# Channel weights loaded as four whole rows per partition, with the contraction index taken as 4p+c

## The chip, the cores and the metric

The kernel runs on one core of one Trainium2 chip. The metric is device time of one execution in microseconds (us), and the time given for a kernel is the median of its runs. Times of single instructions come from one profiled execution and are counted from the start of its span.

## The reference

Two layers follow each other. The first is a linear attention with 8 batches, 8 heads, 576 positions and 64 channels a head. The second takes its output as x with 8 x 576 x 512 elements, mixes the lowest 64 frequencies of every channel with complex weights of their own, and ends in a product over channels:

```python
q_p, k_p = (phi(q), phi(k))                       # phi(x) = elu(x) + 1
kv = np.einsum('bhsd,bhse->bhde', k_p, v)
z = np.sum(k_p, axis=2)
num = np.einsum('bhsd,bhde->bhse', q_p, kv)
den = np.einsum('bhsd,bhd->bhs', q_p, z)[..., None] + 1e-06
x = num / den                                     # heads side by side: [8, 576, 512]

X = np.fft.rfft(x, axis=1)
Yr = np.einsum('bmd,mde->bme', Xr, w_r) - np.einsum('bmd,mde->bme', Xi, w_i)   # m < 64
Yi = np.einsum('bmd,mde->bme', Xr, w_i) + np.einsum('bmd,mde->bme', Xi, w_r)
y = np.fft.irfft(Y, n=S, axis=1)
u = x + y
return u + np.maximum(u @ w_ch, 0.0)              # w_ch: [512, 512]
```

The mode weights w_r and w_i are 64 x 512 x 512 float32 each, 134 MB in all. The channel weights w_ch are 512 x 512 float32, 1 MB. This document is about how w_ch lies in the on-chip memory.

## The kernel before

**Stages.** From 0 to about 112 us the kernel loads q, k and v, forms the attention for each batch (`turn_q`, `sum_kv`, `form_x`), and takes the Fourier transform of x as a product with a table (`transform`, L349), with the result placed by `place_x` for the mode products. From then on it walks through 32 pairs of modes (`mode_pair`, L465; the last one is `last_pair`, L490). Pair p multiplies by its weights in 16 matmuls (`product`, L432, into PSUM tile P), copies P to the f16 tile ys (`evacuate`, L447, on VectorE for even p and on ScalarE for odd p), and turns ys into rows of modes with four matmuls against a small table pick_sb (`picks`, L455). The pieces of ys, 128 columns each, are the stationary operand there.

**Weights.** The mode weights come through GpSimd's DMA queue, with a cast from float32 to bfloat16, 1 MB written for each half of a pair (`w_load`, L119; `w_load_last`, L131, in smaller pieces). Five pairs have buffers of their own at the start; later ones share two buffers, so the load of pair p+2 is issued when the product of pair p is done. The channel weights are loaded once, by L529, on the same queue behind the first five pairs, with a cast to float16, into wch16: `[128, 4, 512]`, 128 partitions of 4 pieces. The table pick_sb follows it (L531).

**Other work between the products.** The list `work` holds the rest in a fixed order, and `work_slot` takes so many items of it in the middle and at the end of each pair; `share` says how many. The instructions are pinned to the order of the program (`pin`). For each tile t of 128 rows, `fold` adds the inverse transform of the first 32 modes to x and writes a float16 copy x16w; `turn_x` (L698) transposes it in four pieces of 128 channels into xTw; `channel_product` (L707) multiplies xTw with wch16 and keeps the result as E0. For later modes, `early_rows` (L665), `form_z` (L728), `form_y` (L739) and `ahead_rows` (L920) turn the transposed spectrum into rows (y) and into rows times w_ch (z), and `fold_lead` uses the first two batches' rows. `keep_warm` (L419) adds matmuls whose result nobody reads.

**The end.** `last_pair` multiplies the very last mode the other way round (L518): its weights are the stationary operand, in 32 pieces of 128 columns, and the result y_last lands transposed. After that, L978 to L989 transpose the last rows of y (into last_y, halves copied by ScalarE at L979 and VectorE at L980) and form z, L990 and L767 add the inverse transform to all tiles, ScalarE takes the maximum with zero, VectorE adds, and the rows are stored.

**The index that the change concerns.** In every product with wch16 the 512 contracted channels are split into four pieces of 128. Before, piece c holds channels 128c to 128c+127, and partition p of piece c holds channel 128c + p. Where a transposed operand is made, it takes 128 adjacent columns; where rows are made from it, the four pieces are put side by side.

Of the kernel before, what the change touches and what calls it, by code (L numbers as in the profile page):

```python
# [43 lines left out]
def kernel(  # L44
# [10 lines left out]
    nc = tc.nc  # L55
# [5 lines left out]
    NDC = D // 128  # L61
    NJJ = 4
    NDW = 4 * NDC
    NDL = NDW // 2
# [6 lines left out]
    RA = 2 * B * NA  # L71
# [11 lines left out]
    id16 = const.tile([128, 128], F16, name="id16")  # L83
    fwd_sb = const.tile([128, 5, 2 * NM], F16, name="fwd_sb")
    pick_sb = const.tile([128, 32], F16, name="pick_sb")
    wch16 = const.tile([128, NDC, D], F16, name="wch16")
# [21 lines left out]
    pin = tc.keep_in_program_order  # L108
    PIECES = (slice(0, 2), slice(2, 4), slice(4, 6), slice(6, 7), slice(7, 8))
    HALVES = [slice(0, 64), slice(64, 128)]  # L110

    LAST = NM // 2 - 1

    def w_load(p: int, half: int, pool, tag: str, bufs: int):
        if half == 0:
            w_in[p] = pool.tile([128, NDW, D], BF16, tag=tag, bufs=bufs, name=f"w{p}")
        two = (moe_w_r, moe_w_i)[half][2 * p : 2 * p + 2]
        pin(
            nc.gpsimd.dma_start(  # L119
                out=w_in[p][half::2], in_=two.rearrange("g (r dc) e -> (g r) dc e", dc=NDW)  # L120
            )
        )

    def w_load_last(pool, tag: str, bufs: int):
        w_in[LAST] = pool.tile([128, NDW, D], BF16, tag=tag, bufs=bufs, name=f"w{LAST}")
        for g in range(2):
            for half in range(2):
                rows_in = (moe_w_r, moe_w_i)[half][NM - 2 + g].rearrange("(p dc) e -> p dc e", dc=NDL)
                for dcs in PIECES if (g, half) == (1, 1) else (slice(0, NDL),):
                    dst = w_in[LAST][half::2, g * NDL + dcs.start : g * NDL + dcs.stop]  # L130
                    pieces.append(pin(nc.gpsimd.dma_start(out=dst, in_=rows_in[:, dcs, :])))  # L131
# [279 lines left out]
    def w_get(p: int):  # L411
        if p not in w_in and p == LAST:
            w_load_last(wpool, "w", W_KEEP)
        elif p not in w_in:
            for half in range(2):
                w_load(p, half, wpool, "w", W_KEEP)
        return w_in[p]
# [9 lines left out]
    def work_slot(p: int, name: str):  # L427
        for _ in range(slots.get((p, name), 0)):
            if work:
                work.pop(0)()  # L430

    def product(P, x, n: int, w, dc: int, n_dc: int):  # L432
        c = dc % NDC * 32
        pin(
            nc.tensor.matmul(  # L435
                P[c : c + n, :], x, w[:, dc, :],
                start=(dc < NDC), stop=(dc >= n_dc - NDC), tile_position=(0, c),
                skip_group_check=True,
            )
        )  # L440

    def set_diagonal(p: int):
        for h in range(2):
            src = xt_v[HALVES[h], :, :, :, p].rearrange("p c t b -> p c (t b)")
            pin(nc.vector.tensor_copy(out=xz[p % 2][HALVES[h], :, h, :], in_=src))  # L445
# [9 lines left out]
    def picks(kk: int, st, n: int):  # L455
        for ec in range(NDC):
            pin(
                nc.tensor.matmul(  # L458
                    yt_ps[:, ec, kk % 8 : kk % 8 + n, :].rearrange("p m n -> p (m n)"),
                    st[:, ec * 128 : ec * 128 + 128],  # L460
                    pick_sb[:, 0 : n * 2 * B],
                )
            )

    def mode_pair(p: int):  # L465
# [5 lines left out]
        for dc in range(NDW):  # L471
            product(P, xz[p % 2][:, dc].rearrange("p h n -> p (h n)"), 32, w, dc, NDW)
        if p + 1 < LAST:
            set_diagonal(p + 1)
# [15 lines left out]
    def last_pair():  # L490
        xl = ystage.tile([128, NDL, 2 * B], BF16, name="xl")
        for h in range(2):
            src = xt_v[:, (2 * h + 1) * NDC : (2 * h + 2) * NDC, :, :, LAST]
            pin(
                nc.vector.tensor_copy(
                    out=xl[:, h * NDC : h * NDC + NDC], in_=src.rearrange("p c t b -> p c (t b)")
                )
            )
        w = w_get(LAST)
        kk = NM - 2  # L500
        ahead_rows()
        work_slot(LAST, "start")
        P = psW.tile([128, D], F32, tag="P", bufs=2, name=f"P{kk}")
        for dc in range(NDL):
            n = 32 if dc < NDC else 2 * B
            product(P, xt_cols(dc, kk, n), n, w, dc, NDL)
        st = evacuate(kk, P)
        work_slot(LAST, "mid")
        picks(kk, st, 1)
        pin(nc.vector.tensor_copy(out=Y8[:, :, NA, :], in_=yt_ps[:, :, NA, :]))  # L510
        ahead_gathers()
        keep_warm(3)
        y_last = psW.tile([128, NDC, 2 * B], F32, tag="P", bufs=2, name="y_last")
        for piece in PIECES:
            for dc in range(piece.start, piece.stop):
                for ec in range(NDC):
                    pin(
                        nc.tensor.matmul(  # L518
                            y_last[:, ec, :], w[:, NDL + dc, ec * 128 : ec * 128 + 128], xl[:, dc, :],
                            start=(dc == 0 and ec == 0), stop=(dc == NDL - 1), skip_group_check=True,  # L520
                        )
                    )
            keep_warm(WARM[piece.stop])
        nc.vector.tensor_copy(out=Y8[:, :, NL - 1, :], in_=y_last)

    while pending:
        w_next()
    tc.keep_in_program_order(
        nc.gpsimd.dma_start(out=wch16, in_=moe_w_ch.rearrange("(c p) j -> p c j", p=128))  # L529
    )  # L530
    tc.keep_in_program_order(nc.gpsimd.dma_start(out=pick_sb, in_=pick_dr.ap()))  # L531
    psA_ctx.close()
# [18 lines left out]
    rows = [Y8[:, ec].rearrange("p m n -> p (m n)") for ec in range(NDC)]  # L551
# [38 lines left out]
    YZ = [YZ_all[:, b] for b in range(B)]  # L590
# [74 lines left out]
    def early_rows(b: int):  # L665

        r = 2 * NF
        y_ps = bank(f"ye{b}", [128, NDC, 128], F16)
        for ec in range(NDC):
            yt = YE_T[:, ec].rearrange("p m (t b) -> p (m t) b", b=B)[:, :, b]  # L670
            pin(nc.tensor.transpose(y_ps[:r, ec, :], yt, id16))
        YE[b] = ye_slots()[:, b % 2, :]
        pin(nc.vector.tensor_copy(out=YE[b][:r], in_=y_ps[:r].rearrange("p c r -> p (c r)")))

    ye_at: list = []

# [21 lines left out]
    def turn_x(t: int):  # L698

        x16 = x16w.pop(t)  # L700
        xT_ps = bank(f"xTp{t}", [128, NDC, 128], F16)
        for c in range(NDC):
            pin(nc.tensor.transpose(xT_ps[:, c, :], x16[:, c * 128 : c * 128 + 128], id16))  # L703
        xTw[t] = sW.tile([128, NDC, 128], F16, tag="xTw", bufs=2, name=f"xTw{t}")
        pin(nc.vector.tensor_copy(out=xTw[t], in_=xT_ps))  # L705

# [32 lines left out]
    def form_y(b: int):  # L739

        y_ps = bank(f"yp{b}", [128, NDC, 128], F16)
        for ec in range(NDC):
            pin(nc.tensor.transpose(y_ps[:, ec, :], late_rows(ec, b), id16))
        pin(nc.vector.tensor_copy(out=YZ[b][:, 0, :], in_=y_ps.rearrange("p c r -> p (c r)")))

    def fold_lead(t: int):

# [170 lines left out]
    ahead = sW.tile([128, 2, D], F16, tag="rows", bufs=1, name="rows_ahead")  # L918

    def ahead_rows():  # L920

        pin(nc.vector.tensor_copy(out=Y8[:, :, 0:NA, :], in_=yt_ps[:, :, 0:NA, :]))
        ya_ps = psW.tile([128, NDC, 128], F16, tag="P", bufs=2, name="ya_ps")
        za_ps = psW.tile([128, D], F32, tag="P", bufs=2, name="za_ps")
        for ec in range(NDC):
            pin(nc.tensor.transpose(ya_ps[:, ec, :], rows[ec], id16))
        for ec in range(NDC):
            pin(
                nc.tensor.matmul(
                    za_ps, rows[ec], wch16[:, ec, :], start=(ec == 0), stop=(ec == NDC - 1)  # L930
                )
            )
        pin(nc.scalar.copy(out=ahead[0:RA, 0, :], in_=ya_ps[0:RA].rearrange("p c r -> p (c r)")))
        pin(nc.scalar.copy(out=ahead[0:RA, 1, :], in_=za_ps[0:RA]))

    def late_at(h: int, r0: int, n: int):
# [23 lines left out]
    for n in range(N_PRE):  # L960
# [4 lines left out]
    last = [  # L965
        sW.tile([128, D], F16, tag="x16w", bufs=2, name="last_y"),
        sW.tile([128, NDC, 128], F16, tag="xTw", bufs=2, name="last_z").rearrange("p c r -> p (c r)"),
    ]
    z1_ps = psW.tile([128, NDC, 8, 2 * B], F32, tag="yt", bufs=1, name="z1l")
    y_ps = [  # L970
        psW.tile([128, NDC, 128], F16, tag="P", bufs=2, name=f"ypl{h}")[:, 0 : NDC // 2] for h in range(2)
    ]
# [3 lines left out]
    COLS = [slice(h * hw, h * hw + hw) for h in range(2)]  # L976
    for ec in range(NDC):
        pin(nc.tensor.transpose(y_ps[ec // 2][:, ec % 2, :], rows[ec], id16))  # L978
    pin(nc.scalar.copy(out=last[0][:, COLS[0]], in_=y_ps[0].rearrange("p c r -> p (c r)")))  # L979
    pin(nc.vector.tensor_copy(out=last[0][:, COLS[1]], in_=y_ps[1].rearrange("p c r -> p (c r)")))  # L980
    for h in range(2):
        for ec in range(NDC):
            pin(
# [25 lines left out]
    def sums_of(n: int, tiles_of):  # L1009
        channels(n, tiles_of)  # L1010
        add_inverse(n, 1, tiles_of)
        for i in tiles_of:
# [6 lines left out]
            out=x_of(0), in0=accs[0][:, 0], scalar=0.0, in1=x_of(0), op0=ALU.max, op1=ALU.add  # L1019
# [50 lines left out]
```

## Time and profile before

| What | Value |
|---|---|
| Median of 3 runs | 420.76 us (420.64 to 420.87) |
| The profiled execution | 421.02 us; span of its instructions 419.2 us |
| TensorE matmul busy | 313.1 us, 75% of the span |
| VectorE busy | 231.2 us, 55% |
| ScalarE busy | 155.1 us, 37% |
| GpSimd's DMA queue (casting loads) | 12,688 packets, 81.54 MB, 93.6% of 16 engines' span |
| Read from HBM | 163.93 MB |
| L529, the load of w_ch | 512 KB written; issue 782 ns at 86.88 us; 37.7 us from issue to landing |
| Loads of mode weights, 1 MB written each | 13.1 us (w_r) and 17.5 us (w_i) from issue to landing, at the median |

A line of a group names the source line, the engine, the operation, output and inputs, their shapes, the count, the total busy time and the mean of one in ns, and then how long the engine stood idle before such instructions and what ended that. PE is a matmul and PEld the load of its stationary operand; loads overlap the matmuls before them. A line of the chain or of the timeline starts with the time in us and the duration. The time from a DMA's issue to its landing includes what is queued ahead of it.

### The profile page before, as it was taken

To read this page: it belongs to the slowest core of one execution; us is meant where nothing else is said; L and a number is where in the kernel's file an instruction comes from. 1 tells how busy PE (TensorE), PEld (TensorE's weight loads), DVE (VectorE), ACT (ScalarE), POOL (GpSimd) and SP (SyncE) were. 2 spreads that over 40 slices of the span, in tenths; PEclk is the share of its full clock that TensorE was granted. 3 is DMA by queue.
4 is the path that set the end of the run, shared out by engine and by line. 5 is a ranking of instruction groups with operands and counts; after the bars stand their busy time and mean duration, and the time that the engine had idled before them with its cause. 6 is when DMAs were issued, how large, how long until landed. Compare 5 with 4: busy or idle time off the path is not lost.

```text
span 419.2 us, 7479 instructions
## 1 busy us (share of the span) xinstructions
PE 313.1 (75%) x3143; PEld 162.6 (39%) x3143; DVE 231.2 (55%) x511; ACT 155.1 (37%) x255; POOL 59.1 (14%) x104
## 2 busy tenths in 40 slices
PE   0369997999607774777666686988788877998993
PEld 0257775877301331223222233333333323363421
DVE  4588899695414572464645353464446443532794
ACT  4687797854201020000000233344353423231783
POOL 4222224210011211111111111111111111130200
PEclk9999998579855687555856599899999989799998
DMA  8999999999999999999999999999999999999698
GB/s 217 212 212 217 209 224 203 228 208 222 213 227 205 223 219 208 224 217 209 220 216 214 220 209 220 217 212 220 220 208 220 217 213 220 213 202 177 229 394 331
DMA packets 17229, 93.17 MB, mean 222 GB/s; under 512 B 2284, under 2 KB 3196, under 8 KB 13036
## 3 DMA queue, kind: packets, MB, share of 16 engines
q0 software_dynamic: 12688, 81.54, 93.6%
q1 hardware_dynamic: 4508, 11.16, 7.2%
q8 instruction: 24, 0.39, 0.3%
q14 instruction: 9, 0.07, 0.0%
HBM read 163.93 MB, written 9.44 MB: 414 GB/s over the span
## 4 chain that ended last, share of the span: by engine, by line
DMA 60%; PE 24%; DVE 6%; issue 3%; ACT 3%; POOL 3%; DVEq 0%; ACTq 0%; POOLq 0%
DMA w<-in_moe_w_i_dram 48%; DMA pick_sb<-row_pick 8%; PE P L435 7%; DMA k<-in_k_dram 3%; PE acc L767 3%; PE kvp L260 2%; PE zl L422 2%; PE acc L807 2%; PE eps L713 2%; DVE x L296 1%; POOL w L119 1%; PE z L733 1%; ACT ke L211 1%; PE yb L752 1%; ACT qT L247 1%
## 5 line engine op out<-in xcount | busy, mean ns | idle before, releaser
L435 PE MATMUL P<-w,xz 128*32 128x512 bf16 x496 | 42.9, 479 | 39.2 <-DMA w<-in_moe_w_i_dram 37.0
L452 ACT CAST ys<-P 128x512 f16<-128x512 f32 x15 | 8.8, 586 | 133.7 <-PE P L435 133.7
L422 PE MATMUL zl<-wch,id 128*128 128x512 f16 x177 | 55.9, 466 | 0.0
L119 POOL DMA_DIRECT2D w<-in_moe_w_r_dram x31 | 17.1, 552 | 247.8 <-PE P L435 222.1
L450 DVE CAST ys<-P 128x512 f16<-128x512 f32 x17 | 11.8, 692 | 51.6 <-PE P L435 51.6
L713 PE MATMUL eps<-wch,xTw 128*128 128x512 f16 x144 | 39.7, 402 | 0.0
L435 PEld LDWEIGHTS <-xz 128*32 128x32 bf16 x496 | 12.5, 108 | 64.4 <-DMA w<-in_moe_w_i_dram 40.9
L166 PEld LDWEIGHTS <-qT 64*128 64x128 f16 (+1 forms) x640 | 22.6, 122 | 30.7 <-issue 16.0
L696 ACT CAST x16w<-x_main 128x512 f16<-128x512 f32 x32 | 19.8, 618 | 37.4 <-DVE x_main L694 37.4
L694 DVE TENSOR_TENSOR x_main<-ya,x_main 128x512 f32<-128x512 f32 x32 | 22.0, 689 | 18.4 <-PE ya L690 18.2
L260 PE MATMUL kvp<-vpad,ke 32*128 32x130 f16 x576 | 24.3, 261 | 8.9 <-ACT qT L247 6.0
L445 DVE COPY xz<-xt_c 64x256 bf16<-64x256 bf16 x62 | 23.0, 372 | 11.2 <-PE P L435 10.4
L721 ACT CAST E<-eps 128x512 f16<-128x512 f32 (+1 forms) x40 | 21.2, 540 | 19.0 <-PE eps L713 19.0
L422 PEld LDWEIGHTS <-id 128*128 128x128 f16 x177 | 18.2, 113 | 24.3 <-issue 13.8
L260 PEld LDWEIGHTS <-ke 32*128 32x128 f16 x576 | 22.1, 115 | 10.6 <-issue 8.1
L166 PE MATMUL nw<-kv_sb,qT 64*128 64x65 f16 (+1 forms) x320 | 17.9, 230 | 10.1 <-DVE x_tail L657 4.7
L296 DVE TENSOR_TENSOR x<-num,rd 128x512 f16<-128x512 f32 x32 | 22.1, 692 | 1.1
L240 PE MATMUL qTp<-id,qe 128*128 128x128 f16 x144 | 14.1, 276 | 11.5 <-DVE qe L224 9.5
L458 PE MATMUL yt<-pick_sb,ys 128*128 128x32 f16 (+1 forms) x128 | 8.6, 183 | 17.3 <-DMA pick_sb<-row_pick 9.7
L705 DVE COPY xTw<-xTp 128x512 f16<-128x512 f16 x36 | 15.0, 416 | 11.5 <-PE xTp L703 11.4
L657 DVE TENSOR_TENSOR x_main<-nw,rd 128x256 f32<-128x256 f32 x32 | 11.2, 416 | 17.6 <-PE nw L166 17.6
L211 ACT ACTIVATE qe<-q 128x1152 f16<-128x1152 f16 (+1 forms) x16 | 17.9, 1157 | 8.3 <-DMA q<-in_q_dram 8.2
(129 smaller groups left out, 509.1 us busy)
## 6 DMA issues: line engine op xcount, KB each, us to landing
w<-in_moe_w_r_dram POOLq DMA_DIRECT2D x31, 1024.0 KB, 13.1
w<-in_moe_w_i_dram POOLq DMA_DIRECT2D x31, 1024.0 KB, 17.5
out_dram<-x_main SPq DMA_DIRECT2D x12, 512.0 KB, 3.7
k<-in_k_dram POOLq DMA_DIRECT2D x8, 576.0 KB, 12.8
v<-in_v_dram POOLq DMA_DIRECT2D x8, 576.0 KB, 14.5
q<-in_q_dram POOLq DMA_DIRECT2D x7, 576.0 KB, 12.6
out_dram<-x_main SPq DMA_DIRECT2D x8, 256.0 KB, 3.0
q<-in_q_dram SPq DMA_DIRECT2D x2, 576.0 KB, 4.5
```

Of the source, the lines that this page charges most:

```text
L119: nc.gpsimd.dma_start(out=w_in[p][half::2], in_=two.rearrange("g (r dc) e -> (g r) dc e", dc=NDW))
L166: mm = nc.tensor.matmul(num[hpo][orow, c0 : c0 + 65], qT[rows, hpp, h2, cols], kv_sb[rows, hpp, h2, :])
L211: pin(nc.scalar.activation(out=ev[:, c], in_=heads(nm, b, c), func=AF.Exp))
L260: nc.tensor.matmul(kv_ps[:, h2, 0:130], phi["k", b][r0 : r0 + 32, j // NJ, j % NJ].rearrange("p o d -> p (o d)"), vp[r0 : r0 + 32, :, j, 0 ...
L296: nc.vector.tensor_tensor(out=dst.rearrange("p (o c d) -> p o c d", o=2, c=4), in0=nv[:, :, :, 0:64], in1=rden.unsqueeze(3).broadcast_to([ ...
L422: pin(nc.tensor.matmul(last_ps[0], id16, wch16[:, 0, :]))
L435: nc.tensor.matmul(P[c : c + n, :], x, w[:, dc, :], start=(dc < NDC), stop=(dc >= n_dc - NDC), tile_position=(0, c), skip_group_check=True,)
L445: pin(nc.vector.tensor_copy(out=xz[p % 2][HALVES[h], :, h, :], in_=src))
L694: pin(nc.vector.tensor_tensor(out=x, in0=acc, in1=x, op=ALU.add))
L696: pin(nc.scalar.copy(out=x16w[t], in_=x))
L713: nc.tensor.matmul(e_ps, xT[:, c, :], wch16[:, c, :], start=(c == 0), stop=(c == NDC - 1))
L721: pin(nc.scalar.copy(out=dst, in_=e_ps[:, cols]))
```

## The change

Piece c now holds channels 4p + c. For the load this means that partition p takes rows 4p to 4p+3 of w_ch, which lie next to each other in HBM: 128 runs of 8 KB are read in the place of 512 runs of 2 KB, and 4 KB are written to each partition in one run in the place of four of 1 KB. What is contracted with it follows: where a transposed operand is made, every fourth column is taken (`ec::NDC`, step 4) in the place of 128 adjacent ones, in `picks`, in `last_pair` and in `turn_x`. Where rows are made from the transposed pieces, the copies out of PSUM write every fourth element (`by_ec`, a view of the output with the piece as an outer index), so that the rows themselves have their channels in the old order. The number of instructions stays the same.

```diff
--- before.py
+++ after.py
@@ -110,6 +110,9 @@
     HALVES = [slice(0, 64), slice(64, 128)]
 
     LAST = NM // 2 - 1
+
+    def by_ec(rows):
+        return rows.rearrange("p (r c) -> p c r", c=NDC)
 
     def w_load(p: int, half: int, pool, tag: str, bufs: int):
         if half == 0:
@@ -457,7 +460,7 @@
             pin(
                 nc.tensor.matmul(
                     yt_ps[:, ec, kk % 8 : kk % 8 + n, :].rearrange("p m n -> p (m n)"),
-                    st[:, ec * 128 : ec * 128 + 128],
+                    st[:, ec::NDC],
                     pick_sb[:, 0 : n * 2 * B],
                 )
             )
@@ -516,7 +519,7 @@
                 for ec in range(NDC):
                     pin(
                         nc.tensor.matmul(
-                            y_last[:, ec, :], w[:, NDL + dc, ec * 128 : ec * 128 + 128], xl[:, dc, :],
+                            y_last[:, ec, :], w[:, NDL + dc, ec::NDC], xl[:, dc, :],
                             start=(dc == 0 and ec == 0), stop=(dc == NDL - 1), skip_group_check=True,
                         )
                     )
@@ -526,7 +529,7 @@
     while pending:
         w_next()
     tc.keep_in_program_order(
-        nc.gpsimd.dma_start(out=wch16, in_=moe_w_ch.rearrange("(c p) j -> p c j", p=128))
+        nc.gpsimd.dma_start(out=wch16, in_=moe_w_ch.rearrange("(p c) j -> p c j", c=NDC))
     )
     tc.keep_in_program_order(nc.gpsimd.dma_start(out=pick_sb, in_=pick_dr.ap()))
     psA_ctx.close()
@@ -670,7 +673,7 @@
             yt = YE_T[:, ec].rearrange("p m (t b) -> p (m t) b", b=B)[:, :, b]
             pin(nc.tensor.transpose(y_ps[:r, ec, :], yt, id16))
         YE[b] = ye_slots()[:, b % 2, :]
-        pin(nc.vector.tensor_copy(out=YE[b][:r], in_=y_ps[:r].rearrange("p c r -> p (c r)")))
+        pin(nc.vector.tensor_copy(out=by_ec(YE[b][:r]), in_=y_ps[:r]))
 
     ye_at: list = []
 
@@ -700,7 +703,7 @@
         x16 = x16w.pop(t)
         xT_ps = bank(f"xTp{t}", [128, NDC, 128], F16)
         for c in range(NDC):
-            pin(nc.tensor.transpose(xT_ps[:, c, :], x16[:, c * 128 : c * 128 + 128], id16))
+            pin(nc.tensor.transpose(xT_ps[:, c, :], x16[:, c::NDC], id16))
         xTw[t] = sW.tile([128, NDC, 128], F16, tag="xTw", bufs=2, name=f"xTw{t}")
         pin(nc.vector.tensor_copy(out=xTw[t], in_=xT_ps))
 
@@ -741,7 +744,7 @@
         y_ps = bank(f"yp{b}", [128, NDC, 128], F16)
         for ec in range(NDC):
             pin(nc.tensor.transpose(y_ps[:, ec, :], late_rows(ec, b), id16))
-        pin(nc.vector.tensor_copy(out=YZ[b][:, 0, :], in_=y_ps.rearrange("p c r -> p (c r)")))
+        pin(nc.vector.tensor_copy(out=by_ec(YZ[b][:, 0, :]), in_=y_ps))
 
     def fold_lead(t: int):
 
@@ -930,7 +933,7 @@
                     za_ps, rows[ec], wch16[:, ec, :], start=(ec == 0), stop=(ec == NDC - 1)
                 )
             )
-        pin(nc.scalar.copy(out=ahead[0:RA, 0, :], in_=ya_ps[0:RA].rearrange("p c r -> p (c r)")))
+        pin(nc.scalar.copy(out=by_ec(ahead[0:RA, 0, :]), in_=ya_ps[0:RA]))
         pin(nc.scalar.copy(out=ahead[0:RA, 1, :], in_=za_ps[0:RA]))
 
     def late_at(h: int, r0: int, n: int):
@@ -976,8 +979,8 @@
     COLS = [slice(h * hw, h * hw + hw) for h in range(2)]
     for ec in range(NDC):
         pin(nc.tensor.transpose(y_ps[ec // 2][:, ec % 2, :], rows[ec], id16))
-    pin(nc.scalar.copy(out=last[0][:, COLS[0]], in_=y_ps[0].rearrange("p c r -> p (c r)")))
-    pin(nc.vector.tensor_copy(out=last[0][:, COLS[1]], in_=y_ps[1].rearrange("p c r -> p (c r)")))
+    pin(nc.scalar.copy(out=by_ec(last[0])[:, 0:2, :], in_=y_ps[0]))
+    pin(nc.vector.tensor_copy(out=by_ec(last[0])[:, 2:4, :], in_=y_ps[1]))
     for h in range(2):
         for ec in range(NDC):
             pin(
```

## The prediction

> **What bounds the kernel now.** I read the chain that ended last first. From the page:
>
> ```profile
> DMA 60%; PE 24%; DVE 6%; issue 3%; ACT 3%; POOL 3%; DVEq 0%; ACTq 0%; POOLq 0%
> ...
> q0 software_dynamic: 12688, 81.54, 93.6%
> ```
>
> The chain is mostly DMA, nearly all of it mode weights. The DMA row of the 40 slices stands at 9 from slice 2 to 36, so the queue of casting transfers, which carries the channel weights too, never runs dry until about 385 us. A transfer that gets shorter there would bring forward all that follows it.
>
> Next, in the same chain in order of time, where the stream ends and what comes behind it:
>
> ```profile
> 368.66 2.16 PE zl L422 x10
> 370.82 1.01 PE P L435 x16
> 371.82 0.28 issue
> 372.10 2.10 POOL w L131 x4
> 374.21 12.73 DMA w<-in_moe_w_i_dram
> 386.94 0.05 issue
> 386.99 0.36 PE y_last L518 x8
> 387.34 0.23 PE zl L422
> 387.58 0.01 issue
> 387.58 0.36 PE y_last L518 x8
> ```
>
> Up to 386.99 us the transfers set the pace; from the last landing on (about 388.2) TensorE and the stores do, and that end is some 31 us. So only three places can move the time: the length of the stream, the slack of TensorE against the last landings, and the end.
>
> Third, the timeline of PEld around those landings, for the slack:
>
> ```profile
> 378.10 0.53 PEld L422 LDWEIGHTS <-id 128*128 128x128 f16 x3
> 379.06 0.55 PEld L435 LDWEIGHTS <-xz 128*32 128x32 bf16 x16 [0.42 <-DMA w<-in_moe_w_i_dram]
> ...
> 386.98 0.27 PEld L518 LDWEIGHTS <-w 128*128 128x128 bf16 x8 [0.27 <-DMA w<-in_moe_w_i_dram]
> 387.18 0.10 PEld L422 LDWEIGHTS <-id 128*128 128x128 f16 x1
> 387.58 0.26 PEld L518 LDWEIGHTS <-w 128*128 128x128 bf16 x8 [0.31 <-DMA w<-in_moe_w_i_dram]
> ```
>
> TensorE waits for data in all three, but briefly. At 379.06 the 12 keep-warm matmuls before it (from 376.38, at 216 ns by the chain's 2.16 for ten) stream until 378.97: 0.09 us of real slack. At 386.98 it is about 0.3.
>
> Fourth, the groups by shape, for the prices:
>
> ```profile
> L713 PEld LDWEIGHTS <-xTw 128*128 128x128 f16 x144 | 13.1, 102 | 10.3 <-issue 2.3
> L358 PEld LDWEIGHTS <-x 128*128 128x128 f16 x128 | 9.3, 124 | 2.0
> L743 PEld LDWEIGHTS <-YL 128*128 128x128 f16 x32 | 3.4, 150 | 1.5 <-issue 0.5
> L518 PEld LDWEIGHTS <-w 128*128 128x128 bf16 x32 | 1.2, 96 | 1.0 <-DMA w<-in_moe_w_i_dram 0.6 <-issue 0.3
> L450 DVE CAST ys<-P 128x512 f16<-128x512 f32 x17 | 11.8, 692 | 51.6 <-PE P L435 51.6
> L744 DVE COPY YZ_all<-yp 128x512 f16<-128x512 f16 x8 | 3.4, 425 | 9.5 <-PE yp L743 9.5
> ```
>
> **The transfer itself.** 512 rows of 2 KB become 128 runs of 8 KB; on the SBUF side 1,024-byte packets become 4,096-byte ones. The trace records each packet of this queue: at the median 98 ns for 1,024 B, 173 for 2,048, 625 for 8,192, 1,227 for 16,384. By these durations the transfer costs 512 x 98 / 16 engines = 3.14 us now; a 4,096 B packet, on the line between 2,048 and 8,192, takes about 324 ns, and 128 x 324 / 16 = 2.59 us. That is the upper end of the gain: 0.55 us. But packets overlap on an engine. In the windows view the DMA share is 1.15 and the rate 219 GB/s in 119 to 124 us, where the 1,024-byte packets pass, against 0.99 with 211 and 210 GB/s in 100 to 110 and 126 to 136 us. The bytes move no slower while these small packets pass, so the lower end is no gain. A loss is excluded: the bigger packets cost less per KB in every row. I take 0.1 us, near the measured rate, because that counts bytes and not overlapping durations.
>
> The Trainium skill speaks against a gain here: "DMA: Bandwidth & Descriptors", Specifications, puts the least size for line rate at 512 B, and the runs are above it already. By that the term would be 0, and the sum 0.1 us higher. The rate in the windows agrees.
>
> POOL's issue of the transfer (L529, 782 ns against 552 for a mode-weight load) may fall by 0.2 us. Its data move some 32 us after the issue, so nothing sees it. The table pick_sb, queued behind on POOL, lands with the stream; the 9.7 us that L458 waits for it covers no empty queue.
>
> **Strided weight loads.** Three TensorE groups now read 128 columns with a step of 4 elements: picks (L458, 128 loads), the x turns (L703, 144), the last product (L518, 32). The trace has this very form: L358 steps by 4, and alone at full clock it takes 112 to 114 ns (source view, 92 to 94 us), against 96 to 98 without a step; L743 steps by 8 and takes 150. So +17 ns a load by the row of the same step; the bounds are 0 (hidden under the matmul before) and +53 (L743). The turns stream 128 columns and their L358-like neighbours keep the same 219 ns matmul, so nothing shows there. Picks are 4 x 17 = 0.07 us a pair; before 340 us they end in the wait for weights (37.0 us of it at L435). In the last product only the 4 loads after the last landing are bare: 4 x 17 = +0.07 us (0 to 0.21).
>
> On the step the Trainium skill says, in "SBUF — State Buffer", section "Door 1: The DMA port swizzle", that a 16-byte line needs two hits to read at full rate, so bf16 may step by up to 8 for free. By it these loads cost nothing and the sum would be 0.07 us lower. The rows differ: step 4 costs 17 ns, step 8 over 50, and I go by the rows.
>
> **Strided copies out of PSUM.** On VectorE, 8 copies at L673, 8 at L744, half a row at L980; on ScalarE L933 and L979. They write f16 two bytes at a time, 8 apart. No row shows that form of this size: the packed f16 copy takes 416 to 425 ns, the f32 one 692. Bounds +0 and +0.27 us a row; I take +0.27, the row of one element at a time. Sixteen and a half make 4.5 us on an engine that is 55% busy. L673 lies before 330 us, under the wait for weights. L744 is waited for once (PE yb L752, 0.5 us, at 354.8): +0.27 there. The other seven free banks that are not yet asked for. At the end, L980 runs from 389.26 for 292 ns and would end at 389.67; its reader L990 starts at 389.93 behind the z matmuls. If the tracker takes the interleaved halves for an overlap, L980 also waits for L979 (to 389.52) and ends near 389.95; L990 needs 0.22 us and the next matmul waits for last_z until 390.56, so even that is covered. Were the cover gone, it would cost 0.12 us. ScalarE: L247 reads in steps and takes 1,293 ns for 1,152 elements against 1,153 at L211, +12%; on L979 +0.05 us with 0.18 until L989. L933's gather waits for weights until 387.80.
>
> **TensorE late.** What adds up on TensorE from 350 us: 0.27 at L752, and picks of pairs 27 to 30 and of the last, 5 x 0.07 = 0.35. Less 0.09 at 379.06 and about 0.3 at 386.98 leaves up to 0.25 us; the two last y_last groups stretch by 8 x 17 = 0.14 each against 0.17 us of wait between them, so it need not grow but hardly shrinks: 0 to 0.4 with rounding. Part of the 0.27 falls where the clock is at half (354.3 to 361.1), and what is pushed past it runs at full rate. I take +0.1. The mode-weight issue that moves with it (L131 at 372.10) has 16 KB packets queued ahead until 376, so no gap opens.
>
> **Sum.** -0.1 + 0.07 + 0.1 = +0.07 us. The profiled execution took 421.02 us (span 419.2 and 1.8 around it), 0.26 above the median of 420.76; the difference is carried to the median: 420.83, with the rounding of the terms 420.9. All bounds together: -0.55 to +0.73 (0.4 + 0.21 + 0.12). With the 0.12 us by which the runs differ: 420.1 to 421.6.
>
> **Rivals.** A, the packets' own durations count in full and the rest is hidden: 420.2. For it, a stream that never rests; against, 219 GB/s while the small packets pass. B, slower: the clock gate closes once in the end stage. At 350.9 to 354.3 TensorE was busy 1.84 of 3.40 us, and the clock stood at half for the next 6.8; at 378.2 to 381.6 it was busy 2.60 and the clock held. So the point lies between. A longer wait for a copy near 389 to 391 us (busy 3.04 of 3.40) would have to leave TensorE idle by over 0.44 us more. One spell of 3.41 us at half rate in a stage that TensorE sets costs 1.7 us: 422.5. Against it: no idle of that size comes out of the terms above. C, the descriptors stay at one row each: the copies and loads still pay, the transfer gains nothing: 420.9 to 421.0.
>
> **How the numbers follow.** Forecast 0.65, A 0.12, B 0.10, C 0.06, and 0.07 for what I do not see (0.05 of it faster). Two tenths of a per cent, 0.84 us, is about what a measurement of this kernel can tell from no change. Forecast, A and C lie within it: 0.83. B and the rest are slower: 0.12; faster 0.05. The range of the forecast holds A and C too and leaves B out.
>
> **What would show it.** Right: packets of 4,096 B near 320 ns; L458 and L518 loads at 112 to 114 ns; L744 near 690; PE y_last's last group within 0.4 us of where it is; the end stage as long as before. Wrong: a clock digit under 9 in slices 37 to 39 of 40, a rate over 225 GB/s where the transfer passes, or L744 above 700 ns.

## The result, and the profile after

The changed kernel takes 423.4 us (median of 6 runs, 421.92 to 423.98) against 420.73 us before. The ratio is 1.0056, with a 95% interval of 1.0044 to 1.0067: it is slower by 2.7 us by the medians and by about 2.4 us by the ratio, for two of the six runs, at 421.92 and 422.24 us, lie well below the others. Both are well over the 0.84 us that a measurement of this kernel can tell from no change. The profiled execution took 423.67 us with a span of 421.9 us, 2.7 us more than the one before. All lines below line 112 have moved by 3: L518 of before is L521, L744 is L747.

The page first: the clock digits of the 40 slices, of the kernel before and of the changed one, then the casting queue and the share of the chain by engine after the change:

```profile
PEclk9999998579855687555856599899999989799998
...
PEclk9999958999755666665556598899899998999897
...
q0 software_dynamic: 12304, 81.54, 92.8%
...
DMA 63%; PE 21%; DVE 6%; issue 3%; ACT 3%; POOL 2%; DVEq 0%; ACTq 0%; POOLq 0%
```

The queue has 384 packets fewer, which are the 512 that became 128, and its share of time fell from 93.6 to 92.8%. Its bytes are the same. In slice 38 (390.2 to 400.8 us) the clock digit is 8, where it was 9.

Next the chain of work that ended last, around the landing of the last weights (start, duration, what):

```profile
378.75 9.27 DMA w<-in_moe_w_i_dram
388.02 0.14 issue
388.15 0.67 PE y_last L521 x16
388.83 0.23 PE zl L425
389.06 0.25 PE y_last L521 x8
389.31 0.23 PE zl L425
389.54 0.26 PE y_last L521 x8
389.79 0.02 issue
...
390.10 0.61 PE ypl L981 x4
390.71 0.85 PE zl L987 x4
391.56 0.85 PE z1l L987 x4
392.41 0.43 PE y0l L993
```

Before, y_last was in four groups of 8 with waits for a landing between them; its first matmul started at 386.46 us and its last at 388.34. Now all 32 matmuls stand behind one wait and run from 388.15 on. The first and the last group of before, and the first of after, in the timelines of PE:

```profile
386.46 0.35 PE L518 MATMUL y_last<-xl,w 128*128 128x16 bf16 x8
...
388.01 0.49 PE L518 MATMUL y_last<-xl,w 128*128 128x16 bf16 x8
...
388.15 0.67 PE L521 MATMUL y_last<-xl,w 128*128 128x16 bf16 x16 [2.03 <-DMA w<-in_moe_w_i_dram]
```

Behind them, four matmuls of 256 columns (zl, L987) take 0.85 us; in the kernel before, and in the first experiment below, they take 0.44. The load of stationary operands shows the same wait in the timeline of PEld:

```profile
385.16 0.21 PEld L461 LDWEIGHTS <-ys 128*128 128x128 f16 x4 [0.41 <-DVE ys L453]
385.29 0.34 PEld L425 LDWEIGHTS <-id 128*128 128x128 f16 x3
388.12 0.61 PEld L521 LDWEIGHTS <-w 128*128 128x128 bf16 x16 [2.49 <-issue]
388.65 0.10 PEld L425 LDWEIGHTS <-id 128*128 128x128 f16 x1
```

PEld stands idle for 2.49 us ahead of y_last, where the longest wait at this place was about 0.3. The releaser is given as "issue" here, and in the PE row of the same group as the weights' DMA (2.03 us). And the windows view, one stretch of before and then three of after, each of 3.41 us, up to and through the spell of half clock, a time in which the granted clock is 0.50 (busy us and count of PE, PEld, DVE, ACT, POOL; then granted clock, DMA share, GB/s):

```profile
385.02:388.43 3.41, 3.22 (x45) 1.74 (x44) 0.68 (x2) 0.00 (x0) 0.13 (x1) 1.00 0.51 87
...
383.31:386.72 3.41, 2.82 (x21) 0.79 (x19) 0.92 (x2) 0.15 (x1) 0.00 (x0) 1.00 0.72 133
386.72:390.13 3.41, 1.89 (x36) 1.41 (x37) 0.23 (x1) 0.00 (x0) 0.63 (x1) 1.00 0.31 69
390.13:393.54 3.41, 3.38 (x15) 1.99 (x16) 1.39 (x2) 1.52 (x4) 0.43 (x1) 0.50 0.20 68
```

PE is busy 1.89 of 3.41 us in the stretch with the wait, where it was 3.22 before, and in the next one the granted clock is 0.50. So the 2.67 us by which the span grew can be laid out between marks that both traces have:

| Mark | Before | After | Longer by |
|---|---|---|---|
| End of the last weight packet | 387.94 | 387.75 | -0.19 |
| from there to the start of the last y_last matmul | 0.40 | 1.85 | +1.45 |
| from there to the first product with last_z | 2.22 | 3.27 | +1.05 |
| from there to the end of the span | 28.66 | 29.02 | +0.36 |

The packets' ends are read from the packets that the trace records. The second row is the order of work, the third and fourth hold the clock: the last 0.67 us of the spell lies behind the third mark. Nothing ahead of the last landing has become later.

Where the wait comes from can be read in the instruction streams of the two built programs. Each lists, for each instruction, the semaphores that it waits for:

```
y_last matmul        1st   9th   17th   25th   29th    transfers waited for
before                2     1      1      1      1
after                 6     0      0      0      0
```

The two profiles show the same waits: ahead of the first y_last matmul TensorE has three semaphore instructions in the place of one, which is why the profile after counts 7,481 instructions against 7,479 (so their number did not quite stay the same). Apart from this the waits on the engines are the same but for trivial differences. The transfers of the last weights write different rows of one tile, `w`. With 128 adjacent columns, `w[:, NDL + dc, ec * 128 : ec * 128 + 128]`, a matmul is made to wait for the transfer of its own rows. With `w[:, NDL + dc, ec::NDC]` the first matmul is made to wait for all of them, though it reads no element of the later ones. The data that it needs have landed by 386.46 us in the trace before, where it starts then; the wait is put in when the program is built. Why a read in steps is taken to touch the other rows was not looked into.

### The profile page after: what moved, and what is told of

It is laid out like the page before. It is cut to its first block, busy times and chain, and to the rows that moved or that the text cites. A ratio compares the mean times of both kernels' runs of the same rounds, so it can differ in the third digit from the quotient of the medians.

```text
span 421.9 us, 7481 instructions
## 1 busy us (share of the span) xinstructions
PE 314.6 (75%) x3143; PEld 163.6 (39%) x3143; DVE 243.7 (58%) x511; ACT 156.1 (37%) x255; POOL 59.1 (14%) x104
## 3 DMA queue, kind: packets, MB, share of 16 engines
q0 software_dynamic: 12304, 81.54, 92.8%
## 4 chain that ended last, share of the span: by engine, by line
DMA 63%; PE 21%; DVE 6%; issue 3%; ACT 3%; POOL 2%; DVEq 0%; ACTq 0%; POOLq 0%
DMA w<-in_moe_w_i_dram 51%; DMA pick_sb<-row_pick 8%; PE P L438 6%; DMA k<-in_k_dram 5%; PE acc L770 3%; PE acc L810 2%; PE kvp L263 2%; ACT ke L214 2%; POOL w L122 1%; PE zl L425 1%; PE eps L716 1%; DVE x L299 1%; PE z L736 1%; PE xTp L706 1%; PE ya L693 1%
## 5 line engine op out<-in xcount | busy, mean ns | idle before, releaser
L425 PE MATMUL zl<-wch,id 128*128 128x512 f16 x177 | 57.2, 475 | 0.0
L263 PE MATMUL kvp<-vpad,ke 32*128 32x130 f16 x576 | 22.7, 251 | 8.9 <-ACT qT L250 6.1
L263 PEld LDWEIGHTS <-ke 32*128 32x128 f16 x576 | 20.8, 110 | 10.5 <-issue 8.1
L461 PE MATMUL yt<-pick_sb,ys 128*128 128x32 f16 (+1 forms) x128 | 9.7, 191 | 19.3 <-DMA pick_sb<-row_pick 11.9
```

What stands on the lines that cost most here:

```text
L263: nc.tensor.matmul(kv_ps[:, h2, 0:130], phi["k", b][r0 : r0 + 32, j // NJ, j % NJ].rearrange("p o d -> p (o d)"), vp[r0 : r0 + 32, :, j, 0 ...
L425: pin(nc.tensor.matmul(last_ps[0], id16, wch16[:, 0, :]))
```

## The experiments

Two theories stood against each other. Theory W ("theory 1" in the expectations): the loss is the wait for all pieces, by the order of work and by the clock that the idle engine loses. Theory L: it comes from the strided forms themselves, from slower stationary loads or slower copies on the way to the end. Each edit is against the kernel named with it, and each time stands beside that of the kernel before on the same chip.

**The changed kernel with the wait taken off.** Each y_last matmul is declared independent of the transfers that write other rows:

```diff
--- after
-        for piece in PIECES:
+        for k, piece in enumerate(PIECES):
...
-                    pin(
+                    mm = pin(
...
+                    for later in pieces[len(pieces) - len(PIECES) + k + 1 :]:
+                        tc.declare_no_dep(mm.ins, later.ins, reason="rows of another piece")
```

> The changed kernel, with every y_last matmul declared free of the pieces of weights that it does not read. Theory 1 (the strided read makes the first y_last matmul wait for all six transfers of the last weights, 1.2 us of matmuls then stand behind the last landing, and the idle TensorE lets the clock gate close for 3.4 us): first y_last matmul back near 386.5 us, last one near 388.5, no half-rate spell after 361 us, time 420.6 to 421.3. Rival (the strided copies out of PSUM, 1.29 us a row where 0.42 stood, are what costs): 423 or more, as the changed kernel.

Measured: 421.31 us against 420.87, ratio 1.0009 (0.9999 to 1.0018). The ratio leaves out one of the 11 runs, of 606.25 us, whose cause is not known. The chain from the last landing:

```profile
388.07 0.43 PE y_last L521 x8
388.50 0.23 PE zl L425
388.74 0.40 PE y_last L521 x8
389.14 0.23 PE zl L425
389.37 0.34 PE y_last L521 x8
...
390.02 0.40 PE ypl L983 x4
390.41 0.44 PE zl L989 x4
```

Here y_last had begun at 387.56, and its last matmul started 0.49 us after the last weight packet; the four matmuls of zl take 0.44 us, so the clock is whole. This profiled execution took 422.25 us because its last packet came only at 389.03 us, 1.1 us later than in the one before; why that landing moves between 387.5 and 389.0 us from one execution to another was not settled. The strided loads and copies are all still in this kernel: by the ratios (1.0056 and 1.0009) about 2 of the 2.4 us were the wait.

**The kernel before with only the wait added.** Adjacent columns, old load, old copies; the first y_last matmul is made to depend on the last four pieces, which with its own two are all six transfers:

```diff
--- before
+                    if not first:
+                        first.append(mm)
+                        for later in pieces[-4:]:
+                            tc.add_manual_dep(mm.ins, later.ins.name, ..., reason="all pieces first")
```

> The kernel before, with one edit: the first y_last matmul also waits for the last four pieces of the weights. Nothing is strided, the channel weights lie as before. Theory 1: last y_last matmul 1.0 to 1.3 us later than in the kernel before, a half-rate spell near 390 us in most runs, 421.8 without the spell and 423 to 424 with it. Rival (copies, strided loads): 420.7, as before.

Measured: 423.27 us (423.09 to 423.36), ratio 1.0057 (1.0045 to 1.0069), which is the changed kernel's own. Its PE timeline, and its windows:

```profile
384.94 0.81 PE L422 MATMUL zl<-wch,id 128*128 128x512 f16 x3
388.16 0.55 PE L519 MATMUL y_last<-xl,w 128*128 128x16 bf16 x16 [2.41 <-DMA w<-in_moe_w_i_dram]
```

```profile
385.98:389.39 3.41, 1.23 (x34) 1.02 (x35) 0.00 (x0) 0.00 (x0) 0.63 (x1) 1.00 0.31 56
389.39:392.80 3.41, 3.38 (x21) 1.96 (x19) 0.68 (x3) 1.12 (x3) 0.00 (x0) 0.50 0.35 108
```

The wait alone, without any of the strided accesses of the change, makes the idle, the spell at 0.50 and the whole loss. Theory W holds, and what remains is to part the order from the clock.

**The wait filled: a first try.** More keep-warm matmuls ahead of y_last in the changed kernel:

```diff
--- after
-        keep_warm(3)
+        keep_warm(13)
         y_last = psW.tile(...)
```

> The changed kernel with 13 keep-warm matmuls in the place of 3 ahead of y_last, which fill about 2.2 us of the 2.5 us that TensorE waits there. Theory 1 with the clock gate: the wait for all pieces stays, the half-rate spell goes, 421.8 to 422.2, and the runs lie within 0.3 us of each other. If the idle TensorE does not decide the spell: 423.4 with a spread of 2 us, as the changed kernel.

Measured: 423.24 us (422.2 to 424.04), ratio 1.0055 (1.0043 to 1.0067), no gain at all. The PE timeline of the profiled run, of 423.24 us, tells why:

```profile
386.39 2.97 PE L425 MATMUL zl<-wch,id 128*128 128x512 f16 x13
389.20 0.68 PE L521 MATMUL y_last<-xl,w 128*128 128x16 bf16 x16
```

The spell is gone, and the way from y_last to the first product with last_z is 2.23 us as before. But in this execution the keep-warm matmuls began at 386.39, 1.07 us later than in the changed kernel's trace (385.32), and y_last began 1.5 us after the last packet, behind them. The filling took from the order what it gave to the clock. Its length had been sized on one execution, and the start of the gap moves.

**The wait filled with fewer.** The same in two kernels, 9 keep-warm matmuls (in the place of 3) in the kernel before with the wait added, and 8 in the changed kernel:

```diff
--- before, with the wait added        --- after
-        keep_warm(3)                   -        keep_warm(3)
+        keep_warm(9)                   +        keep_warm(8)
```

> e2_wait_all with 9 keep-warm matmuls in the place of 3 ahead of y_last: 1.3 of the 2.1 us of its wait are filled, so few that they end before the last landing. If the clock gate closes for want of work in that wait: no half-rate spell after 361 us and 421.7 to 422.2 (only the 1.0 us of matmuls behind the last landing is left). If the spell has another cause: 423.3, as e2_wait_all.

> The changed kernel with 8 keep-warm matmuls in the place of 3 ahead of y_last: e3_filled_wait had 13, and they ran 1.2 us past the last landing and stood in its way. Theory 1 in full (wait for all pieces 1.1 us, half-rate spell 1.2 us): the spell goes, the 1.1 us stay, 421.8 to 422.3. If the filling does not matter to the changed kernel: 423.2, as e10_changed_again.

Measured: 422.02 us, ratio 1.0033 (1.002 to 1.0045), and 422.4 us, ratio 1.0034 (1.002 to 1.0047). In the kernel before with the wait, four of five runs lie between 421.9 and 422.21 us and one at 423.2, where all five of the unfilled one lay above 423. Its PE timeline and windows:

```profile
385.62 2.10 PE L422 MATMUL zl<-wch,id 128*128 128x512 f16 x9
388.15 0.55 PE L519 MATMUL y_last<-xl,w 128*128 128x16 bf16 x16 [0.43 <-DMA w<-in_moe_w_i_dram]
```

```profile
384.22:387.63 3.41, 3.41 (x25) 1.15 (x17) 0.92 (x2) 0.00 (x0) 0.00 (x0) 1.00 0.72 126
387.63:391.04 3.41, 2.90 (x49) 2.21 (x49) 0.52 (x2) 0.69 (x2) 0.63 (x1) 1.00 0.40 119
```

y_last starts at 388.15 as with the wait unfilled, its last matmul 1.64 us after the last packet; but the clock is whole and the next step takes 2.22 us in the place of 3.26. By the medians the clock was 423.27 - 422.02 = 1.25 us of the loss and the order 422.02 - 420.90 = 1.12 us; the two kernels ran on different chips, but their traces say nearly the same, 3.26 - 2.22 = 1.04 us in this step and 0.18 us behind it. In the changed kernel the filling shows less: the profiled run has no spell, but the median lies just above the range expected, and two of six runs still took 423.15 and 423.24 us.

**The changed kernel once more.**

> The changed kernel itself, on the chip of e9_filled_less, to be compared with it: 423.2 to 423.5, with a half-rate spell near 390 us in most runs.

Measured: 422.9 us against 421.0, ratio 1.0048 (1.0031 to 1.0064). That is less than expected: its six runs fall into two groups of three, 422.38 to 422.46 and 423.34 to 423.92. With 8 keep-warm matmuls four and two runs were in the like groups, so on the changed kernel these runs do not tell filled from unfilled. The profiled one took 422.41 and has no spell; the keep-warm matmuls ahead of y_last began at 386.37 there and left 1.00 us idle:

```profile
386.37 0.81 PE L425 MATMUL zl<-wch,id 128*128 128x512 f16 x3
388.18 0.67 PE L521 MATMUL y_last<-xl,w 128*128 128x16 bf16 x16 [1.00 <-DMA w<-in_moe_w_i_dram]
```

Still the last y_last matmul started 1.89 us after the last packet. So in both profiles of the changed kernel the order is paid, and the clock in one: the two groups lie 1.3 us apart, near the 1.25 us found above. That the slower group is the one with the spell is shown by one profile in each (423.67 with, 422.41 without), not for every run. Where the gap starts goes along with earlier spells: in the six traces with one near 340 us the keep-warm matmuls begin at 385.6 to 386.9 us (this one among them), in the six without it at 384.8 to 385.9.

**The load alone.** The kernel before with only the new view of w_ch, so that its products contract channels that do not belong together:

```diff
--- before
-        ... in_=moe_w_ch.rearrange("(c p) j -> p c j", p=128))
+        ... in_=moe_w_ch.rearrange("(p c) j -> p c j", c=NDC))
```

> The kernel before with the new load of the channel weights alone (nothing that is contracted with them follows, so their products are permuted). It prices the transfer: by the packets' own durations 0.55 us less (420.2), by the rate of bytes 0 to 0.1 us less (420.7). Packets of 4,096 B near 324 ns. Both lie within the 0.2% that can be told.

Measured: 420.81 us against 420.9, ratio 1.0003 (0.9994 to 1.0012). In the windows view from 119 to 124 us, where the channel weights pass, before and with the new load:

```profile
119.00:124.00 5.00, 0.00 (x0) 0.00 (x0) 0.00 (x0) 0.00 (x0) 0.00 (x0) 0.50 1.15 219
...
119.00:124.00 5.00, 0.00 (x0) 0.00 (x0) 0.32 (x1) 0.00 (x0) 0.14 (x1) 0.50 0.99 210
```

The DMA share where these packets pass is 0.99, where it was 1.15, and the rate is 210 GB/s against 219. The 128 packets of 4,096 B, 322 ns each at the median, pass from 118.94 to 124.10 us; the 512 of 1,024 B passed from 119.06 to 124.23. The packets' summed durations fall, but the passage takes 5.2 us as before, and from 100 to 136 us both kernels move 216 GB/s: the bytes move no faster.

**The strided loads alone.** Only `picks` and `turn_x` take every fourth column; y_last and the copies stay:

```diff
--- before
-                    st[:, ec * 128 : ec * 128 + 128],
+                    st[:, ec::NDC],
...
-            pin(nc.tensor.transpose(xT_ps[:, c, :], x16[:, c * 128 : c * 128 + 128], id16))
+            pin(nc.tensor.transpose(xT_ps[:, c, :], x16[:, c::NDC], id16))
```

> The kernel before with the step of 4 columns in the stationary operands of the picks and of the turns of x alone, neither in y_last nor in the copies (channels are permuted on the way). Theory 1 (the wait in y_last carries the loss): loads of 111 to 117 ns in the place of 98, hidden, 420.7 to 421.0. Rival (272 strided loads add up, 17 ns each, on a late TensorE): up to 421.3 at most; 423 would overturn theory 1.

Measured: 420.98 us against 420.9, ratio 1.0001 (0.9993 to 1.001). The group of the picks' loads:

```profile
L458 PEld LDWEIGHTS <-ys 128*128 128x128 f16 x128 | 7.5, 119 | 26.8 <-issue 9.2 <-DVE ys L450 8.5 <-ACT ys L452 7.9
```

119 ns each in the place of 101 here, and as much for the turns of x (L703), 272 times over, and nothing of it that can be measured reaches the end.

**The strided copies alone.** Only the writes with a step of 4 elements:

```diff
--- before
-        ... tensor_copy(out=YZ[b][:, 0, :], in_=y_ps.rearrange("p c r -> p (c r)")))
+        ... tensor_copy(out=by_ec(YZ[b][:, 0, :]), in_=y_ps))
         (likewise at L673, L933, L979 and L980)
```

> The kernel before, with the strided writes of the change at L673, L744, L933, L979 and L980 alone (the rows of modes that they make have their channels permuted). Theory 1: the copies cost 1.3 us each and still hide, but for one wait at L752 and the pair at the end: 420.7 to 421.3. Rival (copies): 422.5 to 423.5.

Measured: 421.0 us against 420.87, ratio 1.0015 (1.0002 to 1.0028). The medians lie 0.13 us apart; the ratio is carried by 3 of its 12 runs, at 422.55 to 423.7, of which no profile was taken. The profile is of a run of 420.79 us, where nothing near the end is later than before:

```profile
L747 DVE COPY YZ_all<-yp 128x512 f16<-128x512 f16 x8 | 9.9, 1324 | 5.8 <-PE yp L746 5.8
```

**Both cures together.** The first experiment's declaration, and copies that write adjacent elements and read PSUM in steps instead:

```diff
--- after, each matmul independent of other rows
-        pin(nc.vector.tensor_copy(out=by_ec(YZ[b][:, 0, :]), in_=y_ps))
+        pin(nc.vector.tensor_copy(out=YZ[b][:, 0, :].rearrange("p (r c) -> p r c", c=NDC),
+                                  in_=y_ps.rearrange("p c r -> p r c")))
         (likewise for the other copies; the two at the end write pairs)
```

> The changed kernel with y_last waiting for its own pieces, as in e1_own_pieces, and the copies out of PSUM turned round: they read in steps and write side by side (at the end: in pairs). If the cost of the strided copy lies in the scattered 2-byte writes: L676 and L747 at 0.5 to 0.7 us, and 420.6 to 420.9, no slower than the kernel before. If it lies in any step on either side: 1.3 us again and 421.0 to 421.3 as e1_own_pieces.

Measured: 420.79 us against 420.9, ratio 1.0000 (0.9991 to 1.0009). Its copies:

```profile
L749 DVE COPY YZ_all<-yp 128x512 f16<-128x512 f16 x8 | 5.5, 692 | 8.7 <-PE yp L748 8.7
...
L678 DVE COPY ye_slots<-ye 64x512 f16<-64x512 f16 x8 | 5.5, 682 | 7.0 <-PE ye L676 7.0
```

This is the change as it was meant, and its time is that of the kernel before, within the interval: the larger runs bring nothing that can be measured, and the other costs are hidden or gone. Against the first experiment it is 0.5 us lower in the median, but on another chip and with intervals that overlap, so a price of the scattered copies between 0 and about 0.5 us stays open. No version ran clearly faster than the kernel before.

## Why the prediction was wrong

**The step that failed** is in "Strided weight loads": "In the last product only the 4 loads after the last landing are bare: 4 x 17 = +0.07 us". It priced the new form of access and took the waits of the old one as given; the sum had no term for a wait that the change adds, nor for the clock behind it. All 32 loads are bare, with the matmuls and keep-warms between them: the step is worth +1.45 us by the trace. Of this some 0.2 us is the form, since y_last matmuls now follow each other every 33 ns and not every 25. The same prediction asked what the tracker of dependencies would make of interleaved halves at L980, where no wait was added, and did not ask it of a strided read of a tile that lands in pieces, where each piece has a semaphore of its own.

**Rival B** was the one that came, joined to an order that it did not have. Its mechanism is in the trace: one spell of 3.41 us at half rate in the end stage, after an idle well over the "0.44 us more" that it named as its point. But the idle came from a wait for weights ahead of y_last, and not from a copy near 389 to 391 us, as it supposed. The argument against it, "no idle of that size comes out of the terms above", was true of the terms and failed with them. Its price of 1.7 us was the full half of a spell; 1.05 + 0.36 = 1.41 us was paid in the trace, and 1.25 us by the medians. The prediction's bracket (1.84 of 3.40 us busy closes the gate, 2.60 holds it) is too simple: in the trace of the changed kernel 1.86 us busy from 349.17 to 352.58 us was followed by full clock, 1.93 in the next stretch by a spell. Only the 1.23 us of the kernel with the wait added lies so low that a spell followed every time (last section).

**The transfer.** The packets of 4,096 B take 324 ns at the median, as read off the line between their neighbours, and POOL's issue of the load fell from 782 to 560 ns, 0.22 us as said. The term of -0.1 us is too small to be seen; rival A's -0.55 us lies outside the interval of the load alone (-0.25 to +0.5 us). The choice of counted bytes over summed packet durations was right.

**The strided loads and copies.** In the changed kernel the groups are these, with the count, busy time, mean ns of one and the idle time ahead:

```profile
L676 DVE COPY ye_slots<-ye 64x512 f16<-64x512 f16 x8 | 10.3, 1292 | 7.0 <-PE ye L674 7.0
...
L747 DVE COPY YZ_all<-yp 128x512 f16<-128x512 f16 x8 | 9.9, 1331 | 5.4 <-PE yp L746 5.4
L706 PEld LDWEIGHTS <-x16w 128*128 128x128 f16 x144 | 9.9, 121 | 12.4 <-issue 6.9 <-ACT x16w L699 5.0 <-ACT E L724 0.5
...
L461 PEld LDWEIGHTS <-ys 128*128 128x128 f16 x128 | 7.5, 119 | 28.7 <-issue 11.4 <-DVE ys L453 8.5 <-ACT ys L455 7.5
...
L521 PEld LDWEIGHTS <-w 128*128 128x128 bf16 x32 | 1.4, 117 | 2.7 <-issue 2.5
L936 ACT COPY rows_ahead<-ya_ps 96x512 f16<-96x512 f16 x1 | 1.3, 1295 | 5.9 <-PE ya_ps L929 5.9
```

The loads of `picks` and y_last came out at 119 and 117 ns, 18 and 21 more than before and not 17, and that they are hidden in `picks` and `turn_x` was right. The copies were mis-sized: the bound from above was 692 ns, the row of one element at a time, and L747 takes 1,331, so a bound from a row that reads and writes adjacent elements was no bound. On ScalarE the forecast was +12%, from a row that reads in steps, and L936 went from 582 to 1,295 ns, L982 from 372 to 730. L755 now waits 1.4 us for L747 in all, where it was 0.5. In the profile of the strided copies alone it stayed hidden because the end waits for weights, as argued, though for a term more than three times as large; that run's interval leaves 0.1 to 1.2 us.

**TensorE late** did not show. The matmuls ahead of y_last began at 385.32 in the changed kernel and at 386.37 in its second profile; the start moves by 1 us from one execution to another, more than the 0.1 us that was added up.

**The signs to look for** were the right ones. The clock digit under 9 in slices 37 to 39 and L747 above 700 ns both came, and the first of them points at the place of the loss. The rate over 225 GB/s did not: it was 218 from 119 to 124 us, and 215 from 100 to 136 us, against 216 before.

## What to carry to other kernels

When an access to a tile that lands in pieces is changed, ask first whose transfers the new access will be made to wait for, and read the waits of the built program before pricing its nanoseconds; where they are too many, declare the pieces independent or give each a tile of its own (the latter was not tried). A wait on TensorE of a microsecond or two had two prices here, the work that moves behind the landing (about 1.1 us) and a spell of half clock that may follow it (about 1.25 us). Filling the gap bought back the second alone: with 9 matmuls in the kernel before with the wait; with 13 in the changed kernel the filling ran past the landing and cost about as much as it saved. Where rows have to be interleaved on the way out of PSUM, read in steps and write adjacent elements: 692 ns and not 1,331 a copy, though no time of the whole kernel was shown to hang on it.

## What the runs showed of the hardware

**Spells of the clock keep a raster.** In the changed kernel's trace spells of half clock begin at 301.4, 356.0, 390.1 and 417.4 us: 54.6, 34.1 and 27.3 us apart, each a multiple of 3.41. The other traces have such a raster too, each with a start of its own. Counted on it, the stretch before a spell near the end was busy 1.23 us (wait added), 1.89 (the change) and 2.65 (strided loads alone, whose profiled execution of 421.86 us has a spell at 388.7 without the wait for all pieces). Stretches that no spell followed were busy 2.41 (the change again), 2.53 (8 keep-warms) and more, so no one value parts the two.

All stretches at full clock from 250 to 405 us, in the twelve traces together, say how far the busy time decides. Under 1.46 us busy of 3.41 (25 stretches) each was followed by a spell; from 1.55 to 2.01 us (48) 12 were; above 2.02 us (417) one was, the 2.65. So in the middle something else decides too, which these traces do not show; the ends of matmuls are modelled, which blurs the figures.

The Trainium skill, "TensorE: Matmul & The Clock Gate", section "HAM oscillation — how this bites in real kernels", states the rule as no idle gap of TensorE over some 3.4 us. The runs here are stricter: at y_last 2.03 and 2.41 us of idle were followed by a spell, 0.4 to 1.0 us in four of five traces by none.

**Scattered writes took nearly twice as long as stepped reads.** A copy out of PSUM of 512 f16 elements a partition takes 425 ns with both sides adjacent, 692 with a stepped read and adjacent writes, and 1,331 with adjacent reads and writes 8 bytes apart on VectorE; ScalarE takes 582 in the first two cases and 1,295 in the third. The Trainium skill, "VectorE: DVE Perf Modes", section "What auto-detection actually checks", says that VectorE's packed mode (2×_1P) is taken if every tensor is 16-bit with a step of one. The 425 and 692 ns agree with that; of the second step, from 692 to 1,331 ns, that section says nothing.
